# A delta-rule recurrence and a hardswish MLP on one core: eleven quarter products from block four on, later scores in step 12, a later first relu, joined last stores

## The chip, the cores and the metric

The kernel runs on one core of one Trainium2 chip. The metric is the device time of one execution in microseconds (us), given as the median of the runs; lower is better. The engines are TensorE (PE, with its weight loads listed apart as PEld), VectorE (DVE), ScalarE (ACT), GpSimd (POOL) and SyncE (SP), which here issues almost all DMAs.

## The reference

Two parts, joined by a transposition. B = 4 batches, H = 8 heads, S = 768 tokens, D = 48 per head; the MLP has 3072 tokens, d_model 384 and d_ff 2048. All is fp32.

```python
k_n = k / (norm(k) + 1e-6)
for t in range(S):                       # per batch and head, state is D x D
    y[t] = q[t] @ state
    v_old = state.T @ k_n[t]
    state = state + beta[t] * outer(k_n[t], v[t] - v_old)
x = y as (B*S, H*D)
h = x @ w_in
g = h * clip(h + 3, 0, 6) / 6
out = g @ w_out
```

## The kernel before, in words

**Recurrence.** The tokens are cut into N = 24 steps of C = 32 tokens; one step holds 32 tokens of all four batches, 128 rows. Ahead of its turn, `prep(t)` scales the keys (`kb`, GpSimd, L510), transposes keys and queries on TensorE (`pt`, L524), copies them to `KQ` on ScalarE (L532), multiplies them to scores (`sc`, L547) and masks those into `L` and `LB` on VectorE (L558). `inverse(g)` solves the triangular systems of four steps at a time by some sixty small VectorE operations (L759, L764), with a transposition at either end (L469, L473). `chain(t)` is the recurrence proper: products of the state (`ks`, L806), the residual R (L901, L909), X times R (`pz`, L827), the state's update (`su`, L938, and L956), the output (`py`, `y` at L843, L819 and L863), its transposition (`yt`, L873) and the copy into `xT` (L877).

**MLP.** Two steps make a block of 256 tokens, blocks 0 to 11. Of each block, an up stage makes `g` = hardswish(x w_in) and a down stage makes g w_out. Up to block UF - 1 the up stage is `up`: sixteen units of three matmuls of 256 columns (L994), a relu on ScalarE (L1001) and a min-times on VectorE (L1004). From block UF = 5 on it is `up_by_eleven`, a product scheme in quarters: it takes sums of weight tiles (`weight_sums`, sixteen GpSimd operations at L1030, issued in the down stage of block UF - 1) and sums of token tiles (`token_sums`, four VectorE operations at L1056, at unit 11 of the step that completes the block). It too has sixteen units: `begin(j)` and `end(j)` for eight pairs, nine matmuls a pair (L1066), a copy to `g` on ScalarE (L1080), additions on GpSimd (L1030) and VectorE (L1093, L1097), a copy of one more quarter (L1100), a relu into the tile `o` (L1104) and a min-times (L1107). The tile `o` is one buffer: the relu's result, and the output of the down stage on its way to the stores, use it in turn. From block 2 on, `down_by_seven` makes the down stage by seven quarter products in fourteen units (L1218), with sums of `g` on VectorE (L1204) and of results on GpSimd or VectorE (L1228). `to_dram` issues a store per batch (L1143).

**Order.** Until step 5 the order is a list written out by hand (`ORDER`). From there, each step has fifteen units, 0 to 14. `plan` says which parts of the recurrence come at a unit (`ch` is the step's chain, `now` the preparation of the step six later); behind it each unit takes one unit of the MLP (`take(units)`), and some inverse operations (`fill`) whose pace follows `mode["of"]`, `USED` and `mode["mean"]`. An up stage begins at unit 12 of an odd step, so block 4's has step 10 inside, block 5's step 12. In a steady step, `now` has its key copy at unit 1, its query copy at unit 2, its scores at unit 4 and L and LB at unit 5; `ch` has X times R at unit 4 and the state's update at unit 8.

**PSUM.** `ring("pm", ...)` gives four banks to the MLP's and most of the recurrence's products, `ring("pc", ...)` two to `ks`, `sc` and `su`; a new tile takes the bank whose reader was issued first.

Of the kernel before, what the change touches and what calls it, by code (L numbers as in the profile page):

```python
# [14 lines left out]
ACTF = mybir.ActivationFunctionType  # L15
# [29 lines left out]
def kernel(  # L45
# [21 lines left out]
    nc = tc.nc  # L67
    B, H, S, D = q.shape
    DM, FF = moe_w_in.shape
    C, DP = 32, 64  # L70
    P = B * C
    assert P == 128 and S % C == 0 and D <= DP and H % 2 == 0
    N = S // C
# [6 lines left out]
    CB = 2  # L80
# [14 lines left out]
    def rows(b):  # L95
        return slice(C * b, C * b + C)
# [59 lines left out]
    def read(*keys):  # L156
        for key in keys:
            past.add(("read", key))
            reads.setdefault(key, len(reads))
# [53 lines left out]
    for j, value in enumerate((1.0, -1.0)):  # L213
        m = mask2[:, j, :]
        for b in range(B):
            nc.gpsimd.memset(mask2[rows(b), j, :], value)
            nc.gpsimd.affine_select(
                out=mask2[rows(b), j, :], in_=mask2[rows(b), j, :], pattern=[[1, C]],
# [96 lines left out]
    for i, n in enumerate((0, 1, 2, 3, 4, 5, 0, 1, 3, 4, 5, 0, 1, 5, 0, 1)):  # L315
        s, f = weights[i][0].shape[1:]
# [458 lines left out]
    xTs, outs, zs = {}, {}, {}  # L775
# [11 lines left out]
    def chain(t, whole=True):  # L787
# [49 lines left out]
        def output(Z=None):  # L837

            if t > 0:
                needs(("turned", t - 1))  # L840
            y = work.tile([P, DM], FP32, name="y", bufs=1)
            if t > 0:
                nc.scalar.activation(  # L843
                    out=by_pair(y[:]), in_=even, func=ACTF.Copy, scale=parity[:, 1, 1:2]
                )
                past.add(("even", t))
                if ("R", t) in past:
                    read(("ks", t, 0))
                yield 1
                plus(y[:], odd, parity[:, 0, 1:2], y[:])  # L850
                read(*(("ks", t, i) for i in range(2)))
                yield
            needs(("Z", t))
            Z = zs.pop(t)
            ring("pm", NPM, ("py", t))
            py = psM.tile([P, 512], FP32, name="py", tag=slot["pm"])
            of_heads(py, lambda b: b ^ 1, lambda h: LB[:, he(h), :], Z)
            past.add(("BZ", t))
            yield
            if t == 0:  # L860
                nc.scalar.activation(out=y[:], in_=py[:, 0:DM], func=ACTF.Copy)
            else:
                nc.vector.tensor_tensor(out=y[:], in0=y[:], in1=py[:, 0:DM], op=ALU.add)  # L863
            read(("py", t))
            yield
            blk, cc = divmod(t, CB)
            if cc == 0:
                needs(*([("up", blk - 2)] if blk >= 2 else []))
                xTs[blk] = work.tile([128, NKT, TB], FP32, name="xT")
            ring("pm", NPM, ("yt", t))  # L870
            pt = psM.tile([128, NKT, P], FP32, name="yt", tag=slot["pm"])
            for s in range(NKT):
                nc.tensor.transpose(pt[:, s, :], y[:, s * 128 : (s + 1) * 128], ident[:])  # L873
            past.add(("turned", t))
            yield 1
            read(("yt", t))
            nc.scalar.activation(  # L877
                out=xTs[blk][:, :, cc * P : (cc + 1) * P], in_=pt[:], func=ACTF.Copy
            )
            past.add(("seam", t))  # L880
            yield

# [11 lines left out]
        else:  # L894
# [5 lines left out]
            for e in range(2):  # L900
                nc.vector.scalar_tensor_tensor(  # L901
                    out=Rp[:, e].rearrange("p (a w) -> p a w", w=D), in0=even[:, e],
# [4 lines left out]
            if whole:  # L907
                yield
            nc.vector.scalar_tensor_tensor(  # L909
                out=Rp, in0=odd.rearrange("p e a w -> p e (a w)"), scalar=parity[:, 1, 0:1],  # L910
# [43 lines left out]
        for i, x in enumerate(su):  # L954
            sv = state[:, 2 * i : 2 * i + 2].rearrange("p b a w -> p b (a w)")
            nc.vector.tensor_tensor(  # L956
                out=sv, in0=sv, in1=x[:, :, 0 : NP * D], op=ALU.subtract
# [57 lines left out]
                past.add(("up", blk))  # L1015
            yield

    UF = 5
    S1, S2, S4 = (sums_in[:, i] for i in range(3))

    def w_tiles(s, i):
# [26 lines left out]
    def token_sums(blk):  # L1048
        if blk < UF or ("seam", blk * CB + 1) not in past:
            return  # L1050
# [8 lines left out]
    def up_by_eleven(blk):  # L1059
        needs(("sums", blk))  # L1060
        B11, T3x, B21, B22, _, _ = x_tiles(blk)
        B3 = xTs[blk][:, 2].rearrange("p (i c) -> p i c", c=P)
        phs, ready = {}, {}

        def mm(ph, n, w, x, start=False, stop=False):
            nc.tensor.matmul(  # L1066
                ph[:, n], lhsT=w, rhs=x, start=start, stop=stop, skip_group_check=True
            )

        def begin(j):  # L1070
            key = ("ph", blk, "by", j)
            ring("pm", NPM, key)
            ph = phs[j] = psM.tile([128, 4, P], FP32, name="ph", tag=slot["pm"])
            mm(ph, 0, W11[:, j], B11, start=True)
            mm(ph, 1, S1[:, j], T1x)
            mm(ph, 2, W21[:, j], T3x)
            mm(ph, 3, S2[:, j], T2x)
            gs[blk, j] = g_all[:, 2 * j : 2 * j + 2]
            gt = gs[blk, j].rearrange("p i (t c) -> p (i t) c", c=P)
            nc.scalar.activation(out=gt, in_=ph[:], func=ACTF.Copy)  # L1080
            plus_minus(gt[:, 3:1:-1], gt[:, 0:2], gt[:, 3:1:-1], ALU.add)
            plus_minus(gt[:, 0], gt[:, 0], gt[:, 2], ALU.add)

        def end(j):
            ph = phs.pop(j)
            mm(ph, 0, W12[:, j], B21)
            mm(ph, 1, S4[:, j], B22)
            mm(ph, 2, W22[:, j], T4x)
            mm(ph, slice(0, 2), W13[:, j], B3)
            mm(ph, slice(2, 4), W23[:, j], B3, stop=True)  # L1090
            g = gs[blk, j].rearrange("p i c -> p (i c)")
            gt = gs[blk, j].rearrange("p i (t c) -> p (i t) c", c=P)
            nc.vector.tensor_tensor(  # L1093
                out=gt[:, 1:3], in0=ph[:, 1:3],
                in1=gt[:, 3].unsqueeze(1).to_broadcast([128, 2, P]), op=ALU.add,
            )
            nc.vector.tensor_tensor(out=gt[:, 3], in0=ph[:, 3], in1=gt[:, 0], op=ALU.add)  # L1097

            def first():
                nc.scalar.activation(out=gt[:, 0], in_=ph[:, 0], func=ACTF.Copy)  # L1100
                read(("ph", blk, "by", j))
                ro = mlp.tile([128, CB, DM], FP32, name="o", bufs=1)
                r = ro[:].rearrange("p c m -> p (c m)")[:, 0 : 2 * TB]
                nc.scalar.activation(out=r, in_=g, func=ACTF.Relu, bias=half, scale=1.0 / 6.0)  # L1104

                def rest():
                    nc.vector.scalar_tensor_tensor(  # L1107
                        out=g, in0=r, scalar=1.0, in1=g, op0=ALU.min, op1=ALU.mult
                    )

                ready[j] = rest

            ready[j] = first
            if j == NPR - 1:
                past.add(("up", blk))

        def go(j):
            if j in ready:
                ready.pop(j)()

        begin(0)
        yield
        begin(1)
        yield
        for j in range(NPR):
            end(j)
            go(j - 1)
            if j + 2 < NPR:
                yield
                begin(j + 2)  # L1130
                go(j)
                yield
            else:
                go(j)
                if j == NPR - 1:
                    go(j)
                yield

    def to_dram(t, o):
        for b in range(B):  # L1140
            r0 = b * S + t * C
            eng = nc.scalar if t >= N - CB and b % 2 else nc.sync
            eng.dma_start(out=out[r0 : r0 + C, :], in_=o[rows(b ^ 1)])  # L1143

    def down(blk, c, f0):

# [139 lines left out]
    def mlp_units():  # L1286
# [21 lines left out]
        for blk in range(1, N // CB):  # L1308
            mode["of"] = "down"
            mode["mean"] = 0.72 if blk + 1 < UF else 0.4  # L1310
            sums = weight_sums() if blk == UF - 1 else iter(())
            for _ in downs(blk):
# [3 lines left out]
            if blk + 1 < N // CB:  # L1316
                mode["of"] = "eleven" if blk + 1 >= UF else "up"
                for n, _ in enumerate((up_by_eleven if blk + 1 >= UF else up)(blk + 1)):
                    if blk + 1 == FIRST and n >= HF:
# [10 lines left out]
    def take(gen, n=1):  # L1330
        for _ in range(n):
            while next(gen, None) == 1:
                pass
# [107 lines left out]
    with tc.manual_schedule():  # L1441
# [10 lines left out]
        fill = inverse_of(2)  # L1452
        loads = iter(())
        left = due = 0
        USED = {"up": 0.42, "eleven": 1.0, "down": 0.7}
        CHAIN = {0: 0.45, 1: 0.75, 2: 0.75, 3: 0.4, 4: 0.4, 6: 0.5, 9: 0.8, 10: 0.6, 14: 0.2}
        for t in range(LS, N):
            g, i = group(t)
            ch = chain_of(t)
            behind = t - LS < LA - LE  # L1460
            first_of = t + min(LA, LE + t - LS)
            now, more, later = (prep_of(first_of + n) for n in range(3))
# [5 lines left out]
            if i == 2:  # L1468
# [3 lines left out]
                1: lambda: (take(ch), take(now)),  # L1472
                2: lambda: (take(ch), take(now), take(gens["q"], 4)),
                3: lambda: take(ch),
                4: lambda: (take(ch), take(now)),
                5: lambda: take(now),
                6: lambda: take(now),
                8: lambda: take(ch),
                9: lambda: take(ch),
                10: lambda: take(ch),  # L1480
# [7 lines left out]
            ready = (2, 0) if behind or i == 2 and t - LS == LA - LE else (1, 6)  # L1488
# [62 lines left out]
```

## Time and profile before

| | |
|---|---|
| median of the runs | 667.11 us (666.32 to 667.86, 3 runs) |
| profiled execution | 665.93 us, span 664.1 us |
| TensorE clock granted | 0.974 of full speed, mean |
| busy: PE, PEld, DVE, ACT, POOL | 96%, 86%, 73%, 41%, 31% of the span |
| DMA queues | q1 20.9% of 16 engines' span |
| the chain that ended last | PE 90%, DVE 3%, DMA 2%, SPq 2% |

The profile is of one execution; its times are from the start of its span, in us. The chain of waits goes back from the last instruction, at each step to what released it or to the instruction before it on its engine; "issue" is a stretch in which the engine waited for nothing that the profile shows. In the timeline a bracket gives the idle time before an instruction and what ended it. A matmul in fp32 stands in the records twice, so "x18" in a chain piece is nine matmuls for `ph`.

### The profile page before, as it was taken

Reading aid. Unit: us, or ns where it says so; the run is one execution under the profiler, and the core shown is the slowest. Engines: PE = TensorE matmul, PEld = TensorE weight load, DVE = VectorE, ACT = ScalarE, POOL = GpSimd, SP = SyncE. Lnnn points to the kernel's source line nnn. Section 1 sums busy time; section 2 is a strip of 40 time slices with the busy share of each in tenths; the row PEclk is TensorE's granted clock in tenths of the full one; section 3 lists DMA queues with packets and bytes.
Section 4 is the critical chain, followed back from the end, with each engine's and each line's share of the span. In section 5 each row is a group of like instructions: output and inputs, shape, how many; then the busy total and the mean of one; then the engine's idle time right before and its main releaser. Section 6 shows DMA issues by size and latency. Waiting matters only on the chain.

```text
span 664.1 us, 26330 instructions
## 1 busy us (share of the span) xinstructions
PE 636.2 (96%) x11544; PEld 568.1 (86%) x11544; DVE 487.1 (73%) x1146; ACT 272.1 (41%) x532; POOL 203.5 (31%) x320
## 2 busy tenths in 40 slices
PE   2769999999999999999999999999999999999997
PEld 1658987776789989989989999999999999999997
DVE  4899867898555697657979748989658998456353
ACT  5897679331233143142144244244244144153350
POOL 6531112003511320562254354064052241331430
PEclk9659999999999999999999999999999999999999
DMA  7897246212140030041030030020020020000000
GB/s 175 206 236 197 76 98 161 49 28 41 23 83 8 10 66 3 2 85 27 2 74 3 2 74 3 3 61 2 3 50 2 2 50 1 23 19 2 25 1 25
DMA packets 88499, 33.27 MB, mean 50 GB/s; under 512 B 80160, under 2 KB 83232, under 8 KB 88384
## 3 DMA queue, kind: packets, MB, share of 16 engines
q1 hardware_dynamic: 88128, 31.29, 20.9%
q8 instruction: 91, 1.49, 0.9%
q10 hardware_dynamic: 256, 0.30, 0.2%
q14 instruction: 24, 0.20, 0.1%
HBM read 26.84 MB, written 4.72 MB: 48 GB/s over the span
## 4 chain that ended last, share of the span: by engine, by line
PE 90%; DVE 3%; DMA 2%; SPq 2%; ACT 1%; issue 1%; POOL 0%; ACTq 0%; DVEq 0%; POOLq 0%
PE po L1218 28%; PE ph L1066 20%; PE ph L994 16%; PE po L1154 6%; PE ks L806 3%; PE pt L524 3%; PE su L938 3%; PE pz L827 3%; PE py L827 3%; PE sc L547 3%; PE yt L873 1%; DMA spare<-in_moe_w_in_dram 1%; PE pi L684 1%; DMA w_out<-in_moe_w_in_dram 1%; SPq L168 1%
## 5 line engine op out<-in xcount | busy, mean ns | idle before, releaser
L1066 PE MATMUL ph<-xT,w_in 128*128 128x128 f32 (+1 forms) x560 | 121.4, 321 | 0.7 <-ACT KQ L532 0.5
L994 PE MATMUL ph<-xT,w_in 128*128 128x256 f32 (+1 forms) x576 | 117.1, 353 | 0.9 <-ACT xT L877 0.6
L1218 PE MATMUL po<-w_out,g 128*128 128x192 f32 x640 | 110.6, 326 | 0.0
L994 PEld LDWEIGHTS ph<-xT,w_in 128*128 128x128 f32 x576 | 95.2, 194 | 13.9 <-ACT xT L877 1.0
L1218 PEld LDWEIGHTS po<-w_out,g 128*128 128x128 f32 x640 | 104.6, 190 | 0.5
L1066 PEld LDWEIGHTS ph<-xT,w_in 128*128 128x128 f32 x560 | 91.1, 191 | 5.9 <-ACT KQ L532 0.7
L1030 POOL TENSOR_TENSOR g<-g 128x256 f32<-128x256 f32 x112 | 67.9, 608 | 83.2 <-ACT g L1080 78.8
L1218 PE MATMUL po<-spare,g 128*128 128x192 f32 x480 | 86.7, 332 | 0.0
L1218 PEld LDWEIGHTS po<-spare,g 128*128 128x128 f32 x480 | 77.2, 190 | 1.8
L1001 ACT ACTIVATE g<-ph,halves 128x256 f32<-128x256 f32 (+1 forms) x96 | 41.0, 436 | 74.2 <-PE ph L994 74.2
L1228 POOL TENSOR_TENSOR o<-o,u 128x192 f32<-128x192 f32 x18 | 13.2, 731 | 175.8 <-ACT o L1225 97.2
L1080 ACT ACTIVATE g<-ph 128x512 f32<-128x512 f32 x56 | 33.4, 597 | 81.8 <-PE ph L1066 81.8
L1204 DVE TENSOR_TENSOR g<-g 128x512 f32<-128x512 f32 x80 | 55.5, 715 | 5.6 <-PE po L1218 5.6
L759 DVE TENSOR_TENSOR pr<-A 128x30 f32<-128x30 f32 (+9 forms) x150 | 57.5, 383 | 2.7
L764 DVE TENSOR_TENSOR A<-A,pr 128x30 f32<-128x30 f32 (+9 forms) x150 | 55.7, 371 | 3.7
L1004 DVE SCALAR_TENSOR_TENSOR g<-g,ph 128x256 f32<-128x256 f32 (+1 forms) x96 | 34.7, 371 | 29.4 <-ACT g L1001 29.0
L356 ACT ACTIVATE spare<-spare,places 128x768 uint16<-128x768 uint16 (+1 forms) x56 | 52.6, 944 | 2.8 <-DMA kf<-in_k_dram 1.7
L1093 DVE TENSOR_TENSOR g<-ph,g 128x256 f32<-128x256 f32 x56 | 23.5, 420 | 38.5 <-PE ph L1066 30.9
L1225 ACT ACTIVATE o<-po 128x192 f32<-128x192 f32 x40 | 13.2, 330 | 83.2 <-PE po L1218 79.6
L1154 PE MATMUL po<-w_out,g 128*128 128x384 f32 x128 | 45.2, 491 | 0.0
L1107 DVE SCALAR_TENSOR_TENSOR g<-o,g 128x512 f32<-128x512 f32 x56 | 40.7, 726 | 5.9 <-ACT o L1104 5.9
L1104 ACT ACTIVATE o<-g,halves 128x512 f32<-128x512 f32 x56 | 40.4, 722 | 8.7 <-DVE g L1107 5.7
(141 smaller groups left out, 989.1 us busy)
## 6 DMA issues: line engine op xcount, KB each, us to landing
kf<-in_k_dram SPq DMA_DIRECT2D x96, 48.0 KB, 2.4
qb<-in_q_dram SPq DMA_DIRECT2D x96, 48.0 KB, 2.8
vf<-in_v_dram SPq DMA_DIRECT2D x96, 48.0 KB, 2.2
out_dram<-o SPq DMA_DIRECT2D x92, 48.0 KB, 1.6
spare<-in_moe_w_in_dram SPq DMA_DIRECT2D x4, 768.0 KB, 5.9
w_out<-in_moe_w_in_dram SPq DMA_DIRECT2D x4, 768.0 KB, 6.0
w_out<-in_moe_w_out_dram SPq DMA_DIRECT2D x4, 768.0 KB, 6.9
spare<-in_moe_w_out_dram SPq DMA_DIRECT2D x4, 768.0 KB, 5.0
```

What stands on the lines that cost most here:

```text
L356: nc.scalar.activation(out=z, in_=z if n else d.bitcast(I16)[:, :, :, 3], func=func, bias=places[:, n : n + 1], scale=scale,)
L759: nc.vector.tensor_tensor(out=pv, in0=A[:, j + 1 :, j].unsqueeze(2).to_broadcast([n, w, j]), in1=A[:, j, 0:j].unsqueeze(1).to_broadcast([n ...
L764: nc.vector.tensor_tensor(out=A[:, j + 1 :, 0:j], in0=A[:, j + 1 :, 0:j], in1=pv, op=ALU.subtract)
L994: nc.tensor.matmul(ph[:, cols], lhsT=w_in[:, s, f * 128 : (f + 1) * 128], rhs=xT[:, s, cols], start=(s == 0), stop=(s == NKT - 1),)
L1001: nc.scalar.activation(out=g, in_=ph, func=ACTF.Relu, bias=half, scale=1.0 / 6.0)
L1030: nc.gpsimd.tensor_tensor(out=out, in0=a, in1=b, op=op)
L1066: nc.tensor.matmul(ph[:, n], lhsT=w, rhs=x, start=start, stop=stop, skip_group_check=True)
L1104: nc.scalar.activation(out=r, in_=g, func=ACTF.Relu, bias=half, scale=1.0 / 6.0)
L1107: nc.vector.scalar_tensor_tensor(out=g, in0=r, scalar=1.0, in1=g, op0=ALU.min, op1=ALU.mult)
L1154: nc.tensor.matmul(pos[c][:], lhsT=gs[blk, f // 2][:, f % 2, c * P : (c + 1) * P], rhs=w_out[:, f, :], start=(f == 0), stop=(f == NFC - 1),)
L1204: nc.vector.tensor_tensor(out=A(f, *out, 4), in0=A(f, *a, 4), in1=A(f, *b, 4), op=op)
L1218: nc.tensor.matmul(ps[n][:], lhsT=A(f - f % 2, *a)[:, f % 2], rhs=b[:, f], start=(f == 0), stop=(f == HF - 1),)
```

## The change

Five edits. `UF` goes from 5 to 4, so that block 4's up stage is made by eleven products, and the weight sums are issued in block 3's down stage. In `up_by_eleven` the first pair's relu, and the min-times behind it, come one unit later than its copy. In step 12 the scores come at unit 6 and L and LB at unit 7. The last two steps copy `xT` with the batches in their natural order, in two instructions, and their outputs are stored by two DMAs of two batches each, one on ScalarE's queue and one on SyncE's, in place of four of one batch.

```diff
@@ chain(t), output(), into xT
             read(("yt", t))
-            nc.scalar.activation(
-                out=xTs[blk][:, :, cc * P : (cc + 1) * P], in_=pt[:], func=ACTF.Copy
-            )
+            xt = xTs[blk][:, :, cc * P : (cc + 1) * P]
+            if t >= N - CB:
+                xt, pt = (x.rearrange("p s (g y c) -> p s g y c", g=2, y=2) for x in (xt, pt[:]))
+                for y in range(2):
+                    nc.scalar.activation(
+                        out=xt[:, :, :, y ^ 1], in_=pt[:, :, :, y], func=ACTF.Copy
+                    )
+            else:
+                nc.scalar.activation(out=xt, in_=pt[:], func=ACTF.Copy)
             past.add(("seam", t))
...
-    UF = 5
+    UF = 4
@@ up_by_eleven, end(j)
             def first():
                 nc.scalar.activation(out=gt[:, 0], in_=ph[:, 0], func=ACTF.Copy)
                 read(("ph", blk, "by", j))
+                if j == 0:
+                    ready[j] = second
+                else:
+                    second()
+
+            def second():
                 ro = mlp.tile([128, CB, DM], FP32, name="o", bufs=1)
                 r = ro[:].rearrange("p c m -> p (c m)")[:, 0 : 2 * TB]
                 nc.scalar.activation(out=r, in_=g, func=ACTF.Relu, bias=half, scale=1.0 / 6.0)
...
                 begin(j + 2)
+                if j == 1:
+                    go(0)
                 go(j)
@@ to_dram
+        if t >= N - CB:
+            by_batch = out.rearrange("(g y s) m -> g y s m", g=2, y=2)
+            for g, eng in enumerate((nc.scalar, nc.sync)):
+                eng.dma_start(
+                    out=by_batch[g][:, t * C : t * C + C, :], in_=o[2 * C * g : 2 * C * g + 2 * C]
+                )
+            return
         for b in range(B):
             r0 = b * S + t * C
-            eng = nc.scalar if t >= N - CB and b % 2 else nc.sync
-            eng.dma_start(out=out[r0 : r0 + C, :], in_=o[rows(b ^ 1)])
+            nc.sync.dma_start(out=out[r0 : r0 + C, :], in_=o[rows(b ^ 1)])
@@ the units of a step
+        APART = (12,)
...
-                4: lambda: (take(ch), take(now)),
-                5: lambda: take(now),
+                4: lambda: (take(ch), take(now, t not in APART)),
+                5: lambda: take(now, t not in APART),
                 6: lambda: take(now),
+                7: lambda: take(now, t in APART),
```

## The prediction

> **What bounds the kernel now.** I read the page's busy shares first, then the chain of waits, then windows by stage, then the timeline where the chain leaves TensorE.
>
> ```profile
> PE 636.2 (96%) x11544; PEld 568.1 (86%) x11544; DVE 487.1 (73%) x1146; ACT 272.1 (41%) x532; POOL 203.5 (31%) x320
> ```
>
> TensorE is full. The chain, from about 200 us on, is a row of matmul pieces (start, length, what). The start of each stage gives its length:
>
> ```profile
> 281.52 3.88 PE ph L994 x18
> 308.35 2.60 PE po L1218 x16
> ...
> 336.21 2.79 DMA out_dram<-o
> ...
> 359.10 2.60 PE po L1218 x16
> ...
> 383.41 3.38 PE ph L1066 x26
> ...
> 396.59 0.26 issue
> ...
> 409.40 2.60 PE po L1218 x16
> ...
> 433.71 3.38 PE ph L1066 x26
> ...
> 459.47 2.60 PE po L1218 x16
> ...
> 622.66 19.47 PE ph L1066 x144
> ```
>
> The up stage of block 4 (`up`, with the recurrence's step 10 and the end of step 9 inside) lasts 308.35 - 281.52 = 26.83 us. In eleven products, block 6 (step 14 inside) takes 25.99, of which 0.26 is a pause ("issue") that waits for nothing shown, and block 7 takes 25.76. A down stage takes 24.31 (359.10 to 383.41), so block 5's up stage began near 308.35 + 24.30 = 332.65 and took 26.45: 0.69 more than block 7's. The only place after 300 us where the chain leaves TensorE for other engines, the tail apart, lies there. The timeline (start, length, engine, what, idle before it) shows it:
>
> ```profile
> 338.73 0.27 ACT L1100 ACTIVATE g<-ph 128x128 f32<-128x128 f32 x1
> 339.84 0.72 ACT L1104 ACTIVATE o<-g,halves 128x512 f32<-128x512 f32 x1 [0.83 <-ACT g L1100]
> 340.46 1.06 ACT L532 ACTIVATE KQ<-pt 128x512 f32<-128x512 f32 x2
> 341.09 0.30 PEld L1066 LDWEIGHTS ph<-xT,w_in 128*128 128x128 f32 x2 [0.72 <-ACT KQ L532]
> ```
>
> The first relu of block 5 writes the buffer `o`, which the stores of block 4 still read: ScalarE stands idle 0.83 us until the last store lands near 339.0 plus its signal, both KQ copies queue behind it, and TensorE's next products wait 0.72 us for a PSUM slot that the first KQ copy frees.
>
> VectorE and GpSimd in the stage that the weight sums move into (the up stage of block 3, columns PE, PEld, DVE, ACT, POOL busy), and the stage that they leave:
>
> ```profile
> 230.40:257.20 26.80, 26.80 (x428) 23.00 (x428) 23.76 (x60) 9.56 (x20) 6.52 (x9) 1.00 0.23 46
> 281.50:308.35 26.85, 26.85 (x430) 23.05 (x428) 16.37 (x40) 9.56 (x20) 15.48 (x23) 1.00 0.36 69
> 433.70:459.50 25.80, 25.80 (x478) 23.45 (x477) 23.04 (x52) 12.92 (x26) 14.49 (x23) 1.00 0.20 41
> ```
>
> **Eleven products in block 4.** `up` has 48 matmuls of 256 columns; the chain's pieces of six records (three matmuls, one unit) take 1.30 us, so 16 units cost 20.74. The last block runs the eleven-product stage undisturbed in 19.47 (144 records, two per matmul, last line above). The bare difference is 1.27. Embedded, with restarts after each small product, it is 26.83 - 25.76 = 1.07 by block 7 and 26.83 - 25.99 = 0.84 by block 6; with a wait like block 5's it would be 0.38. Bounds 0.38 to 1.27. Block 4 stands where block 6 stands (one step inside, same place in the group of four), but the 0.26 pause is tied to no dependency; I take 1.0.
>
> What this adds beside TensorE: per block 8 times 0.42 + 0.29 + 0.73 on VectorE (L1093, L1097, L1107) in place of 16 times 0.42 (L1004), so 11.5 for 6.7, and 1.9 of token sums (330.62 to 332.58 in block 5) in the stage before, under the last product's 2.6 us; ScalarE 8 times 0.60 + 0.27 + 0.72 for 16 times 0.47; GpSimd 8 times 1.25. Block 7 has just that load and VectorE at 23.04 of 25.80 without a TensorE gap, so I cost it at nothing; without that cover, VectorE's extra 6.7 us would fall on the path. The pace of the inverse's steps follows `mode`: room/mean is 1.23/0.72 = 1.71 in `up` before and 0.65/0.4 = 1.63 after, which by its own arithmetic moves one VectorE operation of some 0.4 us later in steps 10 to 13: nothing.
>
> **Weight sums one block earlier.** Sixteen GpSimd operations (0.73 each) are issued in block 3's down stage instead of block 4's. GpSimd runs about a step ahead (they ran from 285 to 304 before, though issued with work of 308 on), so six will now follow the `kb` that ends near 234.55, eight will follow the `mb` of 245.06, and two come after the `o` addition of 267.61. There VectorE works through inverse operations back to back, and it pays for company: while GpSimd ran from 230.49 to 234.55, five operations that read two SBUF tiles took 0.67 to 0.89 in place of 0.36 to 0.39, while L1004, which reads PSUM, kept its 0.41. That is about 0.33 per GpSimd operation; 14 of them make 4.6 us of VectorE delay between 234 and 254. VectorE's idle stretches from 240 to 263 (0.60, 0.33, 0.16, 0.20, 0.56, 0.26, 0.30, 0.95, 0.84) add up to 4.2 us. The inverse's last transpose ends at 266.43 and `pz` of step 9 starts at 267.17, so 0.74 is spare: 4.6 against 4.2 + 0.74. Bounds: nothing, to 4.6 - 0.74 = 3.9 if no idle absorbs anything. The cover is just enough; I take 0.1. The `sq` work of 268.60, behind two more sums, starts 1.4 later; its reductions delay `y` from 277.0 to about 278.0, and the transposes that read it start after 278.6: hidden.
>
> The Trainium skill (SBUF — State Buffer, Who interferes with whom) says that a VectorE instruction with two SBUF inputs and a GpSimd instruction that reads SBUF exclude each other, the later one being blocked to the other's end. By it a whole 0.73 could be lost each time, 14 × 0.73 = 10.2 us, and the step-9 wait would be 5.3 (670.6 in all). The rows above agree in kind, with 0.33.
>
> **First relu a unit later.** In all eight blocks `first` of pair 0 splits: the copy stays, the relu and VectorE's L1107 move one unit (0.9 to 1.5 us) down their queues. In block 5 the first KQ copy now passes ahead of the relu that waits for the store, so the PSUM slot is free by about 339.7 and TensorE's 0.72 wait goes: -0.7 (bounds 0 and -0.75). Behind the waiting relu now stand the second KQ copy, the copy of `begin(3)` and the even copy of `y` (L843), whose next reader is the scores' PSUM bank. In blocks 6 and on, where the relu doesn't wait, relu 1 waits for L1107 of pair 0, now behind R's second half (0.60): block 7 had it at 443.40, and 442.1 + 0.6 + 0.7 gives 443.4 again: nothing.
>
> **Scores of step 12 two units later.** The 64 score matmuls (0.79) only change place. This lifts the bank wait just named. But L and LB (0.42 + 0.41, L558) now come at unit 7, just ahead of `su` at unit 8, whose second bank is the scores' bank. In block 7, VectorE had 2.8 us between LB's end (447.97) and `su` (450.75). With L behind the additions, L1107 and three inverse operations of units 5 and 6, I get LB's end 0.3 before to 0.8 after `su` wants to start. Bounds 0 and +1.1 (all slower forms of L1107 and L764, 1.00 and 0.88, at once); taken +0.2. Moves past no DMA of SP: the `q` loads stay at unit 2.
>
> **The last stores.** Each engine issues one store of 96 KB per half of block 11 in place of two of 48 KB:
>
> ```profile
> 659.67 1.90 SPq L1143 DMA_DIRECT2D out_dram<-o  x4
> 659.68 1.93 ACTq L1143 DMA_DIRECT2D out_dram<-o  x4
> 660.37 0.35 DVE L1228 TENSOR_TENSOR o<-u,po 128x192 f32<-128x192 f32 x1 [0.73 <-PE po L1218]
> ```
>
> The last issue ends at 661.6; the addition ends at 660.72, so one issue per engine could end at 661.2. It saves 0.42 at most, nothing if the same bytes land no sooner; since the first transfers then were running already, I take -0.35. Splitting the `xT` copy of steps 22 and 23 (two of about 0.33, L1225's shape, for 0.49) adds 0.16; the third quarter product that needs it started 0.59 after its sum (622.35 to 622.94): hidden, else +0.3.
>
> **Sum** against this execution: -1.0 + 0.1 - 0.7 + 0.2 - 0.35 = -1.75, from 665.93 (span 664.1 and 1.8 around it) to 664.2. The median of the runs stands 1.18 above the profiled one: 667.11 - 1.75 = 665.36, say 665.4.
>
> **Rivals.**
> 1. Slower: VectorE and GpSimd block each other in the up stage of block 3, and `pz` of step 9 waits for the inverse. For it: VectorE is 89% busy there. Against: 4.2 us of idle before the deadline. With nothing absorbed, +3.8 more: 669.2. It decides once the delay passes 0.74 us; the change turns slower than before when it passes about 2.6.
> 2. The scores' late L holds `su` of step 12 (1.1), and the gain of block 5 is eaten: 665.4 + 0.9 = 666.3. For it: the thin margin above; against: the scores wait for nothing at all now.
> 3. Block 4 gets block 5's wait (0.38 in place of 1.0) or block 5 keeps its own, because the store lands late whatever the order: 666.0 to 666.1.
> 4. The joined stores land no sooner, 0.35 lost: 665.7, within the forecast.
>
> **Chances.** A measurement of this kernel can tell some 0.2%, 1.3 us, from no change; 665.4 is 1.7 below. Forecast as summed, to within 0.4: 0.62; rival 2: 0.14; rival 3: 0.12; rival 1: 0.12, of which a small part stops short of slower. Faster by over 0.2%: 0.62; within: 0.27 (rivals 2 and 3); slower: 0.11. Range: 664.2 (block 4 at 1.27, no cost from scores and sums, the issue's full 0.42, and half a us of spread between runs) to 667.4 (rivals 2 and 3 and part of 1).
>
> **What would show it.** Right: block 4's up stage at 25.8 to 26.0 and block 5's at 25.8; no ScalarE release ahead of L1066; `pz` of step 9 about 7.4 us after that step's `ks`, as now; the last store's issue ending 0.9 us after the last matmul in place of 1.3. Wrong: TensorE waiting for VectorE at `pz` or `ph` between 235 and 268, for L558 at `su` of step 12, or block 4's stage above 26.4.

## The result, and the profile after

The changed kernel takes 673.88 us, median of 6 runs (672.08 to 674.76). The kernel before, run beside it, took 667.43 (6 runs, 666.07 to 670.51). The ratio is 1.0098, interval 1.0076 to 1.0121: slower by 1%, where 665.4, a little faster than before, was forecast. One execution among the experiments, 682.42 us at a granted clock of 0.942 (`UF = 4` alone), counts as slow and is left out of its ratio, not of its median. The profiled execution took 672.08 with a span of 670.3; that of before 665.93 and 664.1.

The page's busy shares, and the chain of waits (start, length, what; the lines that answer to those of before):

```profile
PE 634.1 (95%) x11592; PEld 567.4 (85%) x11592; DVE 495.5 (74%) x1158; ACT 276.8 (41%) x542; POOL 217.7 (32%) x336
```

```profile
281.43 3.38 PE ph L1072 x26
...
307.01 2.60 PE po L1238 x16
...
331.32 3.38 PE ph L1072 x26
...
357.09 2.60 PE po L1238 x16
...
431.45 3.38 PE ph L1072 x26
...
457.38 2.60 PE po L1238 x16
...
621.43 19.47 PE ph L1072 x144
...
659.14 0.35 DVE o L1248
```

TensorE has 2.1 us less to do. Block 4's up stage lasts 307.01 - 281.43 = 25.58 (26.83 before) and block 5's 357.09 - 331.32 = 25.77 (26.45). In block 5 the chain's step by way of the stores is gone. The last block's up stage begins at 621.43, 1.23 ahead of before's 622.66, and takes the same 19.47. So up to there this execution is faster than that of before. The three stages by window (columns PE, PEld, DVE, ACT, POOL busy, then clock, DMA share, GB/s):

```profile
229.94:257.02 27.08, 27.07 (x428) 22.90 (x428) 26.31 (x58) 9.68 (x20) 17.50 (x23) 1.00 0.22 45
281.43:307.01 25.58, 25.58 (x477) 23.49 (x476) 16.60 (x40) 12.82 (x26) 14.03 (x24) 1.00 0.37 72
431.45:457.38 25.93, 25.91 (x476) 23.43 (x476) 21.86 (x52) 12.93 (x26) 14.54 (x23) 1.00 0.20 41
```

In block 3's up stage, the first of the three, GpSimd went from 6.52 to 17.50. VectorE went from 23.76 of 26.80 to 26.31 of 27.08, with no more operations of its own (58 for 60).

Everything lost lies behind the last matmul. The timeline of the tail (start, length, engine, what, idle before it) and the windows behind it:

```profile
658.44 1.61 SPq L1157 DMA_DIRECT2D out_dram<-o  x2
658.45 1.60 ACTq L1157 DMA_DIRECT2D out_dram<-o  x2
659.14 0.35 DVE L1248 TENSOR_TENSOR o<-u,po 128x192 f32<-128x192 f32 x1 [0.73 <-PE po L1238]
```

```profile
661.00:662.00 1.00, 0.00 (x0) 0.00 (x0) 0.00 (x0) 0.00 (x0) 0.00 (x0) 0.77 0.13 34
...
665.00:666.00 1.00, 0.00 (x0) 0.00 (x0) 0.00 (x0) 0.00 (x0) 0.00 (x0) 0.50 0.13 49
```

The last addition ends at 659.49 and the span at 670.3: a tail of 10.81 us. Before, it ended at 660.72 and the span at 664.1: 3.38. The tail costs 7.43, TensorE's end gains 1.23: 6.20, the whole difference of the spans. In the tail the DMA engines have a busy share of 0.13, as much as 2 of 16 would have, at 49 GB/s. The same view of the kernel before:

```profile
661.00:662.00 1.00, 0.00 (x0) 0.00 (x0) 0.00 (x0) 0.00 (x0) 0.00 (x0) 1.00 0.67 177
```

### The profile page after: what moved, and what is told of

The parts are those of the page before. It is cut to its first block, busy times and chain, and to the rows that moved or that the text cites. A ratio compares the mean times of both kernels' runs of the same rounds, so it can differ in the third digit from the quotient of the medians.

```text
span 670.3 us, 26474 instructions
## 1 busy us (share of the span) xinstructions
PE 634.1 (95%) x11592; PEld 567.4 (85%) x11592; DVE 495.5 (74%) x1158; ACT 276.8 (41%) x542; POOL 217.7 (32%) x336
## 3 DMA queue, kind: packets, MB, share of 16 engines
q8 instruction: 91, 1.49, 0.9%
## 4 chain that ended last, share of the span: by engine, by line
PE 87%; DVE 6%; ACT 2%; issue 1%; SPq 1%; DMA 1%; POOL 1%; ACTq 0%; DVEq 0%; POOLq 0%
PE po L1238 28%; PE ph L1072 21%; PE ph L1000 12%; PE po L1174 6%; PE ks L806 3%; PE pt L524 3%; PE su L944 3%; PE py L827 3%; PE pz L827 3%; PE sc L547 2%; PE yt L873 1%; ACT spare L356 1%; PE pi L684 1%; SPq L1163 1%; DVE pr L730 0%
## 5 line engine op out<-in xcount | busy, mean ns | idle before, releaser
L1072 PE MATMUL ph<-xT,w_in 128*128 128x128 f32 (+1 forms) x640 | 139.0, 321 | 0.0
L1036 POOL TENSOR_TENSOR g<-g 128x256 f32<-128x256 f32 (+1 forms) x128 | 79.2, 620 | 92.8 <-ACT g L1086 87.8
L1072 PEld LDWEIGHTS ph<-xT,w_in 128*128 128x128 f32 x640 | 104.0, 191 | 5.9
L1000 PE MATMUL ph<-xT,w_in 128*128 128x256 f32 (+1 forms) x480 | 94.8, 348 | 0.7 <-ACT xT L885 0.6
L1000 PEld LDWEIGHTS ph<-xT,w_in 128*128 128x128 f32 x480 | 77.4, 195 | 10.8 <-ACT xT L885 0.8
L1086 ACT ACTIVATE g<-ph 128x512 f32<-128x512 f32 x64 | 38.2, 597 | 92.0 <-PE ph L1072 92.0
L1099 DVE TENSOR_TENSOR g<-ph,g 128x256 f32<-128x256 f32 x64 | 26.8, 419 | 43.0 <-PE ph L1072 35.5
L1007 ACT ACTIVATE g<-ph,halves 128x256 f32<-128x256 f32 (+1 forms) x80 | 33.4, 428 | 55.1 <-PE ph L1000 55.0
L1119 DVE SCALAR_TENSOR_TENSOR g<-o,g 128x512 f32<-128x512 f32 x64 | 46.6, 728 | 6.8 <-ACT o L1116 6.8
L1116 ACT ACTIVATE o<-g,halves 128x512 f32<-128x512 f32 x64 | 46.2, 723 | 12.0 <-DVE g L1119 9.4
L1072 PE MATMUL ph<-beta_tok,sums_in 128*128 128x128 f32 x256 | 49.5, 275 | 0.0
```

The costliest lines, as they stand in the source:

```text
L1000: nc.tensor.matmul(ph[:, cols], lhsT=w_in[:, s, f * 128 : (f + 1) * 128], rhs=xT[:, s, cols], start=(s == 0), stop=(s == NKT - 1),)
L1036: nc.gpsimd.tensor_tensor(out=out, in0=a, in1=b, op=op)
L1072: nc.tensor.matmul(ph[:, n], lhsT=w, rhs=x, start=start, stop=stop, skip_group_check=True)
L1119: nc.vector.scalar_tensor_tensor(out=g, in0=r, scalar=1.0, in1=g, op0=ALU.min, op1=ALU.mult)
```

## The experiments

Executions of one program differ by some us (666.07 to 670.51 for the kernel before, above), part of it ahead of step 5. Beside each time stands therefore the stretch from the first `ks` of step 5 to that of step 23 in the profiled execution: 449.41 us before, 448.62 after. It holds all edits but the stores, the `xT` copy of step 23 and the later relu of the last block. It comes from one execution of each kernel. "Tail" is from the end of the last addition to the end of the span. The loss was known to lie in the tail; the first four runs ask why, the others what each of the rest is worth.

**Stores of one batch again** (all else as changed, also the natural order in `xT`).

```diff
-            for g, eng in enumerate((nc.scalar, nc.sync)):
-                eng.dma_start(
-                    out=by_batch[g][:, t * C : t * C + C, :], in_=o[2 * C * g : 2 * C * g + 2 * C]
-                )
+            for b in range(B):
+                r0 = b * S + t * C
+                eng = nc.scalar if b % 2 else nc.sync
+                eng.dma_start(out=out[r0 : r0 + C, :], in_=o[rows(b)])
```

> The changed kernel with its last stores cut back to one batch each on two queues (the xT copies of steps 22 and 23 stay split, in natural order). Theory A (the joined stores alone lose, because each runs on 2 of 16 DMA engines): the time from the last VectorE addition's end to the span's end goes from 10.8 us back to 3.4, as before the change, the other four edits keep their 1.2 to 2.0 us, and the median falls to 665.2 to 666.3. Rival (the loss lies in the middle, where block 9 gave back 0.9 us, or in the split xT copies): the median stays above 669 and the tail is no more than 2 us shorter.

666.91 us; ratio to before 0.999 (0.9975 to 1.0006). Stretch 448.99, tail 3.52. Seven us come back while the split `xT` copy stays. The median is 0.6 above the range expected: TensorE's gain of about 1 us is too small for the time to show.

**Joined stores and split `xT` alone** (on the kernel before; the part of the stores is shown, the copy is that of the change).

```diff
+        if t >= N - CB:
+            by_batch = out.rearrange("(g y s) m -> g y s m", g=2, y=2)
+            for g, eng in enumerate((nc.scalar, nc.sync)):
+                eng.dma_start(
+                    out=by_batch[g][:, t * C : t * C + C, :], in_=o[2 * C * g : 2 * C * g + 2 * C]
+                )
+            return
```

> The kernel before with the joined stores and the split xT copies of steps 22 and 23 alone. Theory A: TensorE's end stays at 660.3 and the tail grows by 7.4 us: 674.5 to 675. Rival (middle): 667 to 668.

674.46 us; ratio 1.0128 (1.0097 to 1.016). Tail 10.78. The profiled execution, at 678.7, was among the long ones of this kernel: its stretch, 453.09, has a pause of 2.04 in an issue on SP and a store wait in block 7, so its tail alone is read. These two edits by themselves make the whole loss; as the run before this one keeps the split copy, it is the stores.

**The same two stores, spread.** The rows of the last block are ordered token before batch, so that a store's slowest dimension is 32 tokens instead of 2 batches. Bytes and number of stores are the same.

```diff
-                xt, pt = (x.rearrange("p s (g y c) -> p s g y c", g=2, y=2) for x in (xt, pt[:]))
+                xt = xt.rearrange("p s (g c y) -> p s g y c", g=2, y=2)
+                pt = pt[:].rearrange("p s (g y c) -> p s g y c", g=2, y=2)
...
-            by_batch = out.rearrange("(g y s) m -> g y s m", g=2, y=2)
+            by_token = out.rearrange("(g y s) m -> g s y m", g=2, y=2)
...
-                    out=by_batch[g][:, t * C : t * C + C, :], in_=o[2 * C * g : 2 * C * g + 2 * C]
+                    out=by_token[g][t * C : t * C + C], in_=o[2 * C * g : 2 * C * g + 2 * C]
```

> The changed kernel with the same two joined stores of 96 KB on the same queues, but with the rows of xT's last block ordered token before batch, so that the store's outermost dimension is 32 tokens in place of 2 batches. Theory A (the outermost dimension's size sets how many DMA engines share a store): about 200 GB/s in the last us, a tail of 3.0 to 3.4, median 664.8 to 665.9. Rival B (a store of 96 KB or of 64 partitions is slow as such): tail above 9, median above 672.

665.59 us; ratio 0.9994 (0.9971 to 1.0017). Stretch 448.46, tail 3.35. The tail's first full window:

```profile
661.00:662.00 1.00, 0.00 (x0) 0.00 (x0) 0.00 (x0) 0.00 (x0) 0.00 (x0) 1.00 0.72 200
```

**One store of four batches per half** (slowest dimension 4).

```diff
+            by_batch = out.rearrange("(b s) m -> b s m", b=B)
+            eng = nc.sync if t % CB else nc.scalar
+            eng.dma_start(out=by_batch[:, t * C : t * C + C, :], in_=o)
```

> The changed kernel with all four batches in one store of 192 KB per half, on ScalarE's queue for the half that ends last and SyncE's for the other: outermost dimension 4. Theory A: four engines, about 98 GB/s in place of 49, so that 393 KB take 4.0 us in place of 8.0: tail 6.5 to 7.2, median 668.5 to 670.5. Rival B (size of one store): twice the bytes in one store, no faster than the change or slower, 673 or more.

669.88 us; ratio 1.0036 (1.0018 to 1.0054). Tail 6.42:

```profile
664.00:665.00 1.00, 0.00 (x0) 0.00 (x0) 0.00 (x0) 0.00 (x0) 0.00 (x0) 1.00 0.26 100
```

A slowest dimension of 2 gives a DMA share of 0.13 and 49 GB/s, of 4 gives 0.26 and 100, of 32 gives 0.72 and 200. From 2 to 32 the rate goes up four times with stores of the same size and number; from 2 to 4 it doubles although the stores are twice as large and half as many. So it is neither the size of a store nor their number. Nor is it the packets: by the DMA views of the tail, each of these kernels and that of before moves the block in 256 packets of 1.5 KB. Beside them stand small ones, under 512 B: 2 for each store of the changed kernel, 4 for each store of four batches, 16 for each spread store and each store of before. The block's 393 KB at 49 GB/s are 8.0 us, at 100 GB/s 3.9: with 2.5 to 2.8 us more each, the tails of 10.81 and 6.42. The Trainium skill (DMA: Bandwidth & Descriptors, Why a DMA increments its semaphore by 16 and not by 1) says that a DMA is dealt over the largest number of engines, up to 16, that divides the slowest dimension of both its sides: 2, 4 and 16 here. The three runs agree with it.

**`UF = 4` alone** (on the kernel before).

```diff
-    UF = 5
+    UF = 4
```

> The kernel before with UF = 4 alone. By the trace of the change, block 4's up stage takes 25.6 to 26.0 us in place of 26.83, the weight sums cost 0.3 in block 3's stages (a wait of yt for y), block 5 keeps its wait of 0.7 for the store: median 666.0 to 666.9. Rival (the eleven-product stage of block 4 meets block 5's wait): 667 or more.

668.76 us; ratio 1.0028 (1.0008 to 1.0047): slower, above the 666.0 to 666.9 expected, with the rival's wait in block 4. Stretch 450.37. Steps 9 and 10 together take 50.42, which is 0.72 less than before's 51.14 but more than the 49.99 of the changed kernel: block 4 now has a wait for its stores like block 5's (0.41 on TensorE). Step 12 takes 26.83 (25.66 before), with a pause of 1.63 in its scores. Block 7 has a store wait too: step 16, in which it lies, takes 25.63 (24.98 before).

**The later first relu alone** (on the kernel before).

```diff
+                if j == 0:
+                    ready[j] = second
+                else:
+                    second()
```

> The kernel before with the later first relu alone. Theory: block 5's 0.7 us go, and block 9 gives some 0.9 back, because VectorE does R's second half ahead of the first min-times and falls behind until yt waits for y: 666.5 to 667.5. Rival (block 9's loss was a late store or chance, not the edit): 666.2 to 666.8 and block 9's up stage at 23.9 as before.

666.82 us; ratio 0.9998 (0.9979 to 1.0017). Stretch 449.10. Step 12 falls from 25.66 to 24.91, and step 20, with block 9's up stage, rises from 23.13 to 24.02: in the profiled execution gain and loss nearly cancel.

**Scores of step 12 where they were** (the first experiment's kernel).

```diff
-        APART = (12,)
+        APART = ()
```

> As the run with the old stores, but the scores of step 12 at units 4 and 5 as before. Theory (the scores would wait for the bank that the late y copy reads): 0.3 to 0.6 slower than that run, with TensorE waiting for ScalarE's y or KQ copy ahead of sc near 342. Rival (the move is a loss: su waits for L and LB, 0.3 in the trace of the change): 0.2 to 0.3 faster.

668.15 us; ratio 1.0016 (0.9998 to 1.0034). Stretch 450.45, 1.46 more than with the scores moved; step 12 takes 26.44 in place of 25.00. The timeline of TensorE in step 12:

```profile
342.82 0.76 PE L547 MATMUL sc<-KQ 64*32 64x64 f32 x53
344.81 0.33 PE L547 MATMUL sc<-KQ 64*32 64x64 f32 x11 [1.23 <-issue]
```

Expected was a loss of 0.3 to 0.6 by a wait for a PSUM bank; no bank is waited for. TensorE stops after 53 of the 64 score matmuls for 1.23 us, with nothing released at the end ("issue"); `UF = 4` alone broke at the same matmul.

**The spread stores, and the later relu up to block 5 only.**

```diff
-                if j == 0:
+                if j == 0 and blk <= 5:
...
-                if j == 1:
+                if j == 1 and blk <= 5:
```

> The changed kernel with the wide joined stores and the later first relu in blocks 4 and 5 alone. If block 9's loss comes from the later relu: 0.6 to 1.0 below the run with wide stores alone, 664 to 665. If it is chance: the same within 0.4.

666.23 us, where 664 to 665 was expected; ratio 0.9983 (0.9966 to 1.0000). Stretch 448.31. Step 20 is back at 23.14, but block 7 now has the store wait. In the timeline the relu stands behind an idle ScalarE and TensorE behind the KQ copy; the chain of waits names the landing of the stores (near 440.2) ahead of the relu:

```profile
440.78 0.72 ACT L1117 ACTIVATE o<-g,halves 128x512 f32<-128x512 f32 x1 [0.59 <-ACT g L1107]
...
442.04 0.30 PEld L1073 LDWEIGHTS ph<-xT,w_in 128*128 128x128 f32 x2 [0.48 <-ACT KQ L532]
```

**The same, with the later relu up to block 7.**

```diff
-                if j == 0 and blk <= 5:
+                if j == 0 and blk <= 7:
...
-                if j == 1 and blk <= 5:
+                if j == 1 and blk <= 7:
```

> The changed kernel with the wide joined stores and the later first relu in blocks 4 to 7 alone, the blocks whose steps still prepare keys. By the stage lengths of the runs so far: the 0.9 us of block 9 stay away (as in the run with blocks 4 and 5 alone), and so does the wait of 0.7 for the store that block 7 had in that run. From the ks of step 5 to that of step 23 it takes 447.4 to 447.9 us (before 449.41, the changed kernel 448.62), and the median is 665 to 666.2. Rival (the later relu costs block 7 as much as it saves): no better than the run with blocks 4 and 5 alone.

665.03 us, 12 runs; ratio 0.9974 (0.9957 to 0.9992). Stretch 447.73, tail as with spread stores: faster than the changed kernel, and by 0.26% than before.

**Step 12's `q` loads six units later, scores unmoved** (on the version without `APART`; a single execution, so no interval).

```diff
-                2: lambda: (take(ch), take(now), take(gens["q"], 4)),
+                2: lambda: (take(ch), take(now), take(gens["q"], 4 * (t != 12))),
...
-                8: lambda: take(ch),
+                8: lambda: (take(ch), take(gens["q"], 4 * (t == 12))),
```

> As the run with old stores and the scores of step 12 left at units 4 and 5, but with that step's four q loads issued at unit 8 in place of 2. There TensorE paused 1.23 us after 53 or 54 of the 64 score matmuls and waited for nothing shown; 1.63 at the same matmul in the run with UF = 4 alone. If the pause belongs to the place in TensorE's instruction stream, it is there again, 1 us or more, at the same matmul. If the traffic of the q loads (DMA engines 47% busy in those us) makes it, it falls below 0.4.

666.07 us; stretch 448.93. Step 12 takes 24.97 and the scores stay whole:

```profile
343.50 0.86 PE L547 MATMUL sc<-KQ 64*32 64x64 f32 x64
```

**The sixteen weight sums made twice** (on the kernel before: once more in block 3's down stage, into the same tiles; a single execution).

```diff
-            sums = weight_sums() if blk == UF - 1 else iter(())
+            sums = weight_sums() if blk == UF - 1 else more_sums() if blk == UF - 2 else iter(())
```

> The kernel before with sixteen more GpSimd sums issued in block 3's down stage, at the place where the change issues its weight sums (the real ones stay in block 4's). If VectorE and GpSimd blocking each other is what cost the change 0.26 us between the ks of steps 8 and 9, that stretch goes from 25.54 to about 25.8, with yt waiting for VectorE's y near 252.6. Rival (the 0.26 came with something else of the change): 25.54 again.

667.05 us. Steps 7 and 8 together take 51.40 (51.13 before), step 9 takes 25.70 (25.60). TensorE waits at one place for it:

```profile
253.67 0.31 PEld L873 LDWEIGHTS yt<-ident,y 128*128 128x128 f32 x3 [0.45 <-DVE y L863]
```

**The later `q` loads on the fastest version** (without `APART`).

```diff
-        APART = (12,)
+        APART = ()
...
-                2: lambda: (take(ch), take(now), take(gens["q"], 4)),
+                2: lambda: (take(ch), take(now), take(gens["q"], 4 * (t != 12))),
...
-                8: lambda: take(ch),
+                8: lambda: (take(ch), take(gens["q"], 4 * (t == 12))),
```

> The version with stores spread over 16 engines and the later relu in blocks 4 to 7 only, but with step 12's scores back at unit 4 and its four q loads at unit 8 in place of unit 2. Theory (the pause in the scores of step 12 comes of the load traffic beside them, since TensorE's instructions are the same as in the runs that paused): the 64 score matmuls stay in one piece of 0.86 us, step 12's stretch is 25.0 us, and the time is that of the version with the moved scores, 665.0 us to within 0.7. Rival (the pause goes with the place of the scores in TensorE's instructions, and the single look without it was luck): the piece breaks after 53 matmuls with 1.2 to 1.6 us of issue, step 12's stretch is 26.2 to 26.8, and the time is some 666.4.

667.28 us, 12 runs; ratio 0.9993 (0.9978 to 1.0008). Stretch 449.78, step 12 takes 26.64. The pause is there again, at the same matmul:

```profile
343.88 0.76 PE L547 MATMUL sc<-KQ 64*32 64x64 f32 x53
346.07 0.33 PE L547 MATMUL sc<-KQ 64*32 64x64 f32 x11 [1.43 <-issue]
```

So the theory of the loads fell: moving them doesn't take the pause away. Those four loads began at 343.67 here and at 343.85 in the single execution that didn't pause, almost the same; unmoved they began at 341.98 (the run with the scores where they were) and at 343.16 (`UF = 4` alone). What does go with the pause is a transfer of instructions (16 KB, the DMA view's queue q8 of that name). In the three profiles that pause it runs at 342.5, 343.6 and 343.5, which is 1.1 to 1.2 us ahead of the 53rd matmul's end, and TensorE goes on 2.3 to 2.8 after it. In the one that doesn't pause the last such transfer ran at 340.1, some 4 ahead. Whose instructions they are, and why they came early once, the traces don't show. Nor is the transfer enough: in the changed kernel one ran at 341.5, behind it came large matmuls, and TensorE did not stop. Only one profile of a kernel with `UF = 4` and unmoved scores is without the pause, so this is no proof.

## Why the prediction was wrong, step by step

**The last stores: the step that failed.** The term was -0.35, between -0.42 and nothing; it measured +7.43 in the tail (10.81 against 3.38). The step counted issues and held the transfer for given, "nothing if the same bytes land no sooner". That they could land later was in neither end, and rival 4 made the same mistake. Yet the store's shape, two batches ahead of 32 tokens, stands in the diff, and in the runs above it goes with how many DMA engines work. The prediction's own sign for this step could not tell: the last issue did end 0.95 after the last matmul (660.05 against 659.10) where 0.9 was forecast, and the tail grew all the same. Nor did the earlier issue save time where the stores were spread: two stores per engine leave a tail of 3.35. An issue of 96 KB took 0.52 to 0.68 where the smaller ones took 0.31 to 0.46, and the median landing was 2.3 us in the spread run (SyncE's stores) where the smaller ones had 1.6 to 1.8. The split `xT` copy was hidden, as forecast: from `ks` of step 23 to the last up stage it is 19.22 in both traces.

**The four other edits.** -1.4 was forecast; TensorE ends 1.23 earlier, of which 0.44 is gained ahead of step 5, before any edit acts, and 0.79 in the stretch. That 1.23 is near 1.4 is in part luck. Behind the 0.79 stand a loss of 0.9 at block 9 that the sum did not have, and a gain of 0.42 in step 14, where block 6's pause is gone, against 0.34 lost in steps 15 and 16; the sum had no term for these either.

*Block 4 in eleven products:* -1.0, measured -1.25, within the bounds and near the bare difference of 1.27: the stage has no wait. It seems to need the later relu: with `UF = 4` alone block 4 waits for its stores, rival 3's first half.

*Weight sums:* +0.1, measured +0.25 in block 3's up stage (27.08 against 26.83) and +0.10 in its down stage. Making them twice gave +0.27 and +0.10. The delay is of the kind forecast, but the place named, `pz` of step 9, has no wait; `yt` has, for the output `y`. The 0.10 of the down stage is at `yt` too, which the prediction had as hidden (its loads begin at 278.27 before, not after 278.6): its piece of the chain lasts 0.43 in place of 0.33, in the run with the sums made twice as well. The up stage's wait, in the timeline of after:

```profile
251.99 0.54 DVE L863 TENSOR_TENSOR y<-y,py 128x384 f32<-128x384 f32 x1
...
252.59 0.31 PEld L873 LDWEIGHTS yt<-ident,y 128*128 128x128 f32 x3 [0.41 <-DVE y L863]
```

The addition that makes `y` has a due time before the end of the inverse, which the step looked past. Rival 1's 3.8 did not come. The sums ran where forecast (six, then eight, then two), but VectorE's busy time in that stage grew by 2.55, not 4.6, and its idle time fell from 3.04 to 0.77: it took most of the delay there, as argued.

*Later first relu, block 5:* -0.7, measured -0.68 against this execution of before. The wait itself is not the same each time: TensorE stood 0.72 there before, but 0.31 in the run with the sums made twice and 0.25 in that with joined stores alone, which have this part of the kernel before unchanged (step 12 takes 25.66, 25.25 and 25.20; 24.91 with the relu alone). So 0.7 is the upper end of what these executions show for the edit there. The timeline of after shows the first KQ copy ahead of the relu and no release by it:

```profile
337.39 0.27 ACT L1106 ACTIVATE g<-ph 128x128 f32<-128x128 f32 x1
...
337.55 0.60 ACT L532 ACTIVATE KQ<-pt 128x512 f32<-128x512 f32 x1
...
338.03 0.73 ACT L1116 ACTIVATE o<-g,halves 128x512 f32<-128x512 f32 x1
...
339.31 0.60 ACT L532 ACTIVATE KQ<-pt 128x512 f32<-128x512 f32 x1 [0.55 <-PE pt L524]
```

*"In blocks 6 and on: nothing"* was wrong at block 9. The chain looked at (the second relu behind L1107 behind R's second half) was the right one, but its sum for block 7, which came out even, was taken for all blocks. In block 9, before and then after:

```profile
538.25 0.68 DVE L1107 SCALAR_TENSOR_TENSOR g<-o,g 128x512 f32<-128x512 f32 x1
...
538.85 0.61 DVE L909 SCALAR_TENSOR_TENSOR R<-ks,parity,R 128x384 f32<-128x384 f32 x1
```

```profile
536.13 0.61 DVE L915 SCALAR_TENSOR_TENSOR R<-ks,parity,R 128x384 f32<-128x384 f32 x1
...
536.66 0.68 DVE L1119 SCALAR_TENSOR_TENSOR g<-o,g 128x512 f32<-128x512 f32 x1
...
537.43 0.72 ACT L1116 ACTIVATE o<-g,halves 128x512 f32<-128x512 f32 x1 [0.41 <-DVE g L1119]
...
547.88 0.54 DVE L863 TENSOR_TENSOR y<-y,py 128x384 f32<-128x384 f32 x1
...
548.54 0.31 PEld L873 LDWEIGHTS yt<-ident,y 128*128 128x128 f32 x3 [1.07 <-ACT o L1116]
```

The second relu waits for the min-times, VectorE falls behind, and `yt` stands for 1.07. Its bracket names a relu that ended at 547.89; `y`, which `yt` reads, was ready only at 548.42, and the chain of waits goes by it. Step 20 takes 24.03 in place of 23.13. All seven profiles with the later relu in block 9 have step 20 at 24.02 or 24.03; the seven without it there have 23.13 or 23.14. Limited to block 7, the edit keeps its gain: 447.73 against 448.46.

*Scores of step 12:* +0.2, measured +0.09 (step 12 25.00 in place of 24.91 with the relu alone). `su` is 0.33 late for LB in the changed kernel; so it is in this timeline of the kernel with stores of one batch:

```profile
350.44 0.76 PEld L944 LDWEIGHTS su<-R,bkb 32*64 32x64 f32 x64 [0.33 <-DVE LB L558]
```

So rival 2's wait came at a third of its size. That scores left in place would cost some 1.5 by a pause in which TensorE waits for nothing shown, in three profiles of four, was not foreseen; the move's gain, where it had one, was not "the bank wait".

*The store wait* moves: block 5 before, block 4 with `UF = 4` alone, block 7 with that and with the later relu up to block 5. Taking it from one block is no promise for the next.

## What to carry to other kernels

Before joining stores, read the slowest dimension of the joined shape: in these runs a size of 2 kept 2 of 16 DMA engines at work, 4 kept 4 and 32 all of them. A tail of bytes is to be priced by share and GB/s, not by the number of issues. A term "nothing at worst" wants a reason why no loss is possible. An edit made in eight blocks is to be priced in each kind of block: the later relu paid where KQ copies stand behind a late store, and in block 9, where R does, cost as much.

## What the hardware showed

The same 393 KB went out at 49, 100 and 200 GB/s with a slowest dimension of 2, 4 and 32. On each of the two queues, two stores of 96 KB on all engines leave as long a tail as four of 48 KB: 3.35 against 3.38.

TensorE stopped 1.23 to 1.63 us inside a run of small matmuls, at the same matmul in three programs, while the DMA engines were some half busy (0.54 to 0.56 in the us before) and a 16 KB instruction transfer had run 1.1 to 1.2 us ahead. The Trainium skill (Runtime: NRT & Kernel Launch, Instruction fetch mechanics) says that instructions come in blocks of 16 KiB, fetched while the block before is worked off, mostly hidden. The profile page of the changed kernel agrees on the size for that queue (q8: 91 packets, 1.49 MB). Whether the pause is such a fetch come late stays open.
